# Reordered units and a sorting copy with its step on the write side, in a kernel of a long convolution and a linear attention

## Chip, cores and metric

The kernel runs on one core of a Trainium2 chip. The metric is the device time of one execution in microseconds, given as the median of several runs; a shorter name below for an engine is PE (TensorE), ACT (ScalarE), DVE (VectorE), POOL (GpSimd) and SP (SyncE, whose queue issues every DMA here).

## What is computed

Two independent heads over S = 2048 time points and D = 576 columns, in bfloat16, whose results stand side by side in the output.

```python
# A: shift convolution, then a long convolution by FFT
k_shift = sum(k_pad[:, t:t+S] * shift_k[:, 3-t] for t in range(4))   # k padded by 3
kv  = k_shift * v
y   = irfft(rfft(pad(kv)) * rfft(pad(ssm_k)))[:S]                    # length 2S, per column
out_a = q * (y + kv * ssm_D)
# B: linear attention, 32 heads of 18 columns
q, k, v = split(x @ wqkv)
pq, pk = phi(q), phi(k)              # phi(t) = (t+1 if t>0 else exp(t)) + 1e-6
kv  = einsum("bhsd,bhse->bhde", pk, v);  z = sum_s pk
out_b = ((pq @ kv) / (pq @ z + 1e-6)) @ wo
out = concatenate([out_a, out_b], -1)
```

## The kernel before, in words

Head A does its Fourier transforms as matmuls, for five chunks of columns (ACH: four of 128, one of 64). Time is split as t = 16a + b, so that a transform is a first step over a (128 points, matrices G), a transposition by DMA, a second step over b (16 points, small matrices W0 and W), a product of spectra, and the way back. The units, each with a name that the lists below use (first number the chunk):

- hl (h_load, L438) loads a chunk of the filter ssm_k, columns on partitions, 2048 time points in a row; hd (h_D, L500) adds D to its first point; hT (h_T, L506) brings time point a to the partitions. hT.0 to hT.2 (mode D) do it with 16 TensorE transposes and one DVE copy. hT.3 (mode a, ACT) and hT.4 (mode p, POOL) first sort the row by b with a copy into hp (L518 to L522), and one DMA transpose from SP (L524) then makes hT.
- cv (L477) is the four-tap shift convolution on DVE or POOL, in stages 0 to 3; each letter of its mode is the engine of one operation.
- h1 and u1 (s1, L527) are the first transform step of the filter and of the signal: 8 matmuls into a PSUM bank and an eviction (L308 on ACT, L310 on DVE) into Ch or Cu. ht and ut (tr, L540) transpose them by DMA into Cth and Ctu. h2 and u2 (s2, L548) are the second step, evicted into T and SU.
- pX, pT, pS, pA (prod, L563) are the product of the spectra on DVE or POOL; the mode N leaves a fold out, and i1 then takes more matmuls. i1 (L580) and i2 (L599) go back, with F, which FT (f_T, L610) makes from G by a DMA transpose. st stores.
- sin, ix, io, iw, iv, sw, wk and W make the matrices G and W from sines at the start; wm (one_w, L359) fills a row of the weights with two memsets (L361, L362).

Head B: xl loads x, xd transposes it (PE, or SP with mode T), k, q and qt are the projections (5 matmuls each half, an exp on ACT at L447, a min/max on DVE at L448), G (b_G, L657) is pk^T x with 32 matmuls, whose eviction needs a column that DVE copies first (L651) before ACT evicts (L652); zs, zz, kv, M, den (with the reciprocal, L743), bc and bt (L745, L755; they divide pq by the denominator, on DVE), and o and ol for the output.

The order of all this is written out by hand as a string, ORDER: one word per unit, with a trailing letter for the engine that evicts, and behind the slash the places (buffer slots and one of four PSUM bank pairs, 0 to 3). Each unit's instructions are put on the queues of their engines in this order, and every engine, SP included, works its queue in order. A unit waits for its bank until the eviction of the last unit there is done. Filter rows, hp and hT share one ring of three slots ("h"), Cth and Ctu one of two ("ct").

Of the kernel before, what the change touches and what calls it, by code (L numbers as in the profile page):

```python
# [29 lines left out]


ORDER = """
io ls ix.0.0/0 sin.1.0 wu.1.A/0 wu.2.B/1 dl ix.1.0/1 sin.0.0 hl.0/0 dc/2 hd.0 Wj.A/301 ix.0.1 id xl.2 iw ix.1.1 sin.0.1
hl.1/1 hT.0.D/22 xd.2.DA/030 hd.1 h1.0.0.0.A/11 h1.0.1.0.D/2 hT.1.D/00 wm iv sin.1.1 xl.0 h1.0.0.1.A/3 xd.0.DA/112
h1.0.1.1.A/0 wk lw.1 sw W lw.2 k.11/3 hl.2/1 hd.2 lw.0 k.9/2 k.2/0 k.1/1 k.10/3 kl.0 h1.1.1.1.A/02 k.8/0 cv.0.0.D es
cv.0.1.DD hc h1.1.1.0.A/1 h1.1.0.1.A/3 q.2.1/2 xl.3 q.0.1/0 k.0/1 h1.1.0.0.A/3 ht.0.0/0 qt.0/2 ht.0.1/1 h2.0.1.1.A/00
cv.0.2.PD vl.0/0 cv.0.3.DDD h2.0.1.0.A/3 eps ql.0/1 q.2.0/1 hl.3/2 xd.3.AA/020 q.0.0/3 k.3/2 ht.1.1/1 u1.0.1.1.A/10
k.15/1 u1.0.1.0.A/3 hT.2.D/00 u1.0.0.1.A/2 u1.0.0.0.A/1 cv.1.0.P cv.1.1.DD k.13/3 cv.1.2.DD h2.1.1.1.A/10 h2.1.1.0.A/2
q.3.1/1 h2.0.0.1.A/20 xd.1.T/1 h2.0.0.0.A/3 cv.1.3.DDP q.3.0/2 ut.0.0/1 u2.0.0.0.A/00 q.1.0/3 k.7/1 k.6/0 FT.0.T
u2.0.0.1.A/2 ut.0.1/0 pX.0.0.D/0 qt.1/3 u2.0.1.0.A/11 u2.0.1.1.D/0 k.12/2 u1.1.1.0.A/11 kl.1 k.5/3 u1.1.0.1.A/0  # L40
pX.0.1.D/1 k.14/1 ht.1.0/1 xl.1 u1.1.0.0.A/2 u1.1.1.1.A/3 cv.2.0.D hl.4/1 pT.0.1.D k.4/0 h1.2.1.0.A/02 pS.0.1.D ut.1.1/0
h1.2.1.1.A/1 cv.2.1.DD pT.0.0.P hd.3 pS.0.0.D q.1.1/3 h2.1.0.0.A/32 h2.1.0.1.A/0 G.1/1 cv.2.2.DP h1.2.0.0.A/2 pA.0.1.N
h1.2.0.1.D/0 u2.1.1.1.A/03 zs/01 ut.1.0/1 u2.1.1.0.A/2 pA.0.0.N i1.0.0.0.D/10 i1.0.0.1.A/3 i1.0.1.0.A/1 zz/2
i1.0.1.1.A/0 pX.1.1.D/0 vl.1/0 cv.2.3.DDD ht.2.0/0 pT.1.1.D u2.1.0.1.A/13 u2.1.0.0.A/2 ht.2.1/1 FT.1.T hT.3.a/02 hd.4
G.3/1 cv.3.0.D cv.3.1.DD u1.2.0.0.A/00 lwv pS.1.1.D u1.2.1.1.A/3 G.0/2 cv.3.2.DD u1.2.1.0.A/1 pX.1.0.D/1 pA.1.0.N
u1.2.0.1.A/0 G.4/3 h2.2.1.1.A/22 cv.3.3.DDD h2.2.1.0.A/1 G.2/0 cv.4.0.D i2.0.0/3 h2.2.0.0.A/02 h2.2.0.1.A/1 wom kv/0
ut.2.0/1 i2.0.1/3 h1.3.0.0.A/12 h1.3.1.0.A/1 h1.3.0.1.D/0 h1.3.1.1.A/3 pA.1.1.P ut.2.1/0 u2.2.0.0.D/02 i1.1.1.1.A/01
i1.1.1.0.A/0 u2.2.0.1.A/3 pT.1.0.D cv.4.1.DD den/2 u2.2.1.1.A/11 pS.1.0.N i1.1.0.1.A/0 i1.1.0.0.A/3 lwo M.3.A/1 M.2.A/0
i2.1.1/3 u2.2.1.0.A/1 i2.1.0/0 ht.3.1/1 h2.3.1.1.A/12 hT.4.p/02 u1.3.1.1.A/01 bc.2/32 u1.3.0.1.A/0 u1.3.0.0.A/1 bt/3
M.1.A/0 u1.3.1.0.A/2 h2.3.1.0.D/1 ht.3.0/0 h2.3.0.1.A/33 bc.0/02 st.0 ut.3.0/1 h1.4.1.0.A/11 h1.4.0.1.A/3 h1.4.1.1.A/1  # L50
h2.3.0.0.A/0 bc.3/31 pX.2.0.P/0 pT.2.0.P M.4.A/2 ut.3.1/0 pX.2.1.P/1 h1.4.0.0.A/0 M.0.A/3 bc.1/20 pA.2.0.N pT.2.1.D
pS.2.1.D u2.3.0.0.A/01 u2.3.0.1.A/3 pS.2.0.P cv.4.2.PD cv.4.3.DDD i1.2.0.1.A/02 i1.2.0.0.A/1 ht.4.0/1 pX.3.0.D/0 ql.1/1
o.1.2.AAf/03 pA.2.1.P i1.2.1.1.A/2 o.0.2.AA/10 u1.4.0.0.D/13 i1.2.1.0.D/2 u1.4.1.0.A/1 h2.4.0.1.A/03 u1.4.1.1.D/0
u1.4.0.1.A/1 u2.3.1.1.A/12 u2.3.1.0.A/3 ut.4.0/0 pT.3.0.D h2.4.0.0.A/0 i2.2.1/1 pX.3.1.D/1 pA.3.1.D pS.3.0.D pA.3.0.P
o.1.0.AA/23 pT.3.1.D o.0.0.AAf/10 u2.4.0.0.A/02 u2.4.0.1.D/3 i1.3.0.1.A/11 i2.2.0/0 i1.3.0.0.A/2 st.1 pX.4.0.D/0
pT.4.0.D pA.4.0.D pS.3.1.P i1.3.1.0.A/3 pS.4.0.D i1.3.1.1.A/1 o.1.3.AAs/02 i2.3.0/3 i1.4.0.0.A/01 i1.4.0.1.D/0 i2.3.1/2
o.0.3.DAs/31 i2.4.0/0 i2.4.1/2 st.2 o.1.1.AA/31 ol.0.1/023
"""


# [192 lines left out]
def kernel(  # L253
# [52 lines left out]
    def evict(out, in_, eng):  # L306
        if eng == 'A':
            nc.scalar.activation(out=out, in_=in_, func=ACT.Copy)  # L308
        else:
            nc.vector.tensor_copy(out=out, in_=in_)  # L310
# [195 lines left out]
    def h_T(ci, eng='D'):  # L506
        d0, dc = ACH[ci]
        s = st[ci]
        hv = s['h'][0:dc, :].rearrange("d (a b) -> d b a", b=16)
        if eng in 'DAH':  # L510
            s['hT'] = slot4([128, 16, 128], BF, "hT", "h", 3)
            for b0, n, e in ((0, 8, 'A'), (8, 8, 'D')) if eng == 'H' else ((0, 16, eng),):
                ps = psum.tile([128, n, 128], BF, name="hT_ps")
                for b in list(range(1, n)) + [0]:
                    nc.tensor.transpose(out=ps[:, b, 0:dc], in_=hv[:, b0 + b, :], identity=K.ident[0:dc, 0:dc])
                evict(s['hT'][:, b0:b0 + n, 0:dc], ps[:, :, 0:dc], e)
        else:
            hp = slot4([128, 16, 128], BF, "hp", "h", 3)[0:dc]  # L518
            if eng == 'a':
                nc.scalar.activation(out=hp, in_=hv, func=ACT.Copy)  # L520
            else:
                nc.gpsimd.tensor_copy(out=hp, in_=hv)  # L522
# [372 lines left out]
```

## Time and profile before

| | us |
|---|---|
| median of three runs | 158.77 (158.46 to 159.52) |
| the profiled execution | 159.33 |
| its span, first to last instruction | 157.6 |
| PE busy | 149.6 (95%) |
| DVE busy | 135.8 (86%) |
| ACT busy | 130.5 (83%) |
| POOL busy | 62.0 (39%) |
| ACT's sorting copy (hT.3), one | 4.02 |
| POOL's sorting copy (hT.4, half the partitions), one | 3.93 |

The profile is one execution. Times in its timelines count from the span's start; a row of a timeline is start, length, engine, line, operation, output<-input, shape and count, and in brackets the idle time of the engine before it and what ended that. A row of groups is line, engine, operation, shapes and count, then busy time and mean of one in ns, then idle time before it with its cause.

### The profile page before, as it was taken

The numbers are of one execution on the slowest core, as the hardware profiler recorded it, in microseconds if no ns is written. First come the engines' busy times: TensorE is split into PE (matmuls) and PEld (weight loads), VectorE is DVE, ScalarE is ACT, GpSimd is POOL, SyncE is SP. The second block draws the span as 40 slices with busy tenths as digits, with TensorE's granted clock in tenths as the row PEclk, the third lists the DMA queues.
The fourth block names the chain that finished last, engine by engine and source line by source line (L and its number), as shares of the span: only waits on it lengthen the run. The fifth ranks groups of instructions, "written<-read, shape, count | busy, mean of one in ns | idle before, by whom it ended". The sixth has DMA issues, their size and how long they took to land.

```text
span 157.6 us, 4600 instructions
## 1 busy us (share of the span) xinstructions
PE 149.6 (95%) x1986; PEld 90.3 (57%) x1986; DVE 135.8 (86%) x169; ACT 130.5 (83%) x162; POOL 62.0 (39%) x70
## 2 busy tenths in 40 slices
...
GB/s 86 391 282 188 294 300 186 253 290 266 184 186 225 127 317 264 143 213 324 177 176 176 209 109 144 192 141 146 263 170 148 131 319 186 173 107 189 0 227 198
DMA packets 74315, 31.92 MB, mean 203 GB/s; under 512 B 52090, under 2 KB 73653, under 8 KB 74294
## 3 DMA queue, kind: packets, MB, share of 16 engines
...
q14 instruction: 6, 0.05, 0.1%
...
## 4 chain that ended last, share of the span: by engine, by line
PE 77%; ACT 12%; DMA 3%; DVE 3%; issue 1%; POOL 1%; DVEq 0%; POOLq 0%; ACTq 0%
PE k_ps L455 12%; PE g_ps L661 10%; PE o_ps L783 9%; PE s_ps L536 8%; PE q_ps L464 8%; PE i_ps L593 6%; PE s_ps L559 5%; DMA Ctu<-Cu 3%; PE i_ps L606 3%; PE i_ps L607 2%; ACT V L308 2%; ACT T L308 2%; ACT Cu L308 2%; PE o_ps L775 2%; ACT G L231 2%; PE qt_ps L472 2%
## 5 line engine op out<-in xcount | busy, mean ns | idle before, releaser
L455 PE MATMUL k_ps<-wqk,xT 128*128 128x512 bf16 (+1 forms) x160 | 21.5, 286 | 0.0
L536 PEld LDWEIGHTS <-G 128*128 128x128 bf16 x320 | 17.4, 98 | 3.6 <-issue 2.7
L464 PE MATMUL q_ps<-xT,wqk 128*128 128x512 bf16 x80 | 18.4, 380 | 0.0
L308 ACT ACTIVATE Cu<-s_ps 128x1024 bf16<-128x1024 f32 (+1 forms) x18 | 17.0, 976 | 0.4 <-PE s_ps L536 0.2
L455 PEld LDWEIGHTS <-xT 128*128 128x128 bf16 x160 | 11.4, 98 | 10.5 <-issue 0.3
L308 ACT ACTIVATE T<-s_ps 128x1024 bf16<-128x1024 f32 x17 | 16.8, 1026 | 0.6 <-PE s_ps L559 0.6
L308 ACT ACTIVATE ob<-o_ps 128x576 bf16<-128x576 f32 (+1 forms) x15 | 9.2, 637 | 9.1 <-PE o_ps L775 4.8
L661 PE MATMUL g_ps<-pk,x_sb 128*128 128x512 bf16 (+1 forms) x128 | 16.5, 286 | 0.0
L308 ACT ACTIVATE Ch<-s_ps 128x1024 bf16<-128x1024 f32 (+1 forms) x17 | 15.2, 928 | 1.0 <-PE s_ps L536 1.0
L494 DVE TENSOR_TENSOR at<-at 128x2048 bf16<-128x2048 bf16 (+1 forms) x14 | 15.5, 1109 | 0.5
L308 ACT ACTIVATE SU<-s_ps 128x1024 bf16<-128x1024 f32 x15 | 15.0, 1040 | 1.0 <-PE s_ps L559 1.0
L308 ACT ACTIVATE V<-i_ps 128x1024 bf16<-128x1024 f32 x15 | 14.7, 1039 | 1.0 <-PE i_ps L593 1.0
L783 PE MATMUL o_ps<-wo_M,pqT 128*128 128x512 bf16 (+1 forms) x112 | 14.9, 286 | 0.0
L448 DVE SCALAR_TENSOR_TENSOR pk<-pk,k_ps 128x576 bf16<-128x576 bf16 x16 | 11.8, 751 | 3.4 <-ACT pk L447 3.3
L493 DVE TENSOR_TENSOR at<-k,Wj 128x2048 bf16<-128x2048 bf16 (+1 forms) x13 | 14.7, 1134 | 0.1
L661 PEld LDWEIGHTS <-x_sb 128*128 128x128 bf16 x128 | 8.4, 97 | 8.9 <-issue 1.2
L447 ACT ACTIVATE pk<-k_ps,neg 128x576 bf16<-128x576 f32 x16 | 11.6, 741 | 1.3 <-PE k_ps L455 0.9
L464 PEld LDWEIGHTS <-wqk 128*128 128x128 bf16 x80 | 7.4, 98 | 9.1 <-issue 1.3
L608 DVE TENSOR_TENSOR q<-i_ps,q 128x1024 bf16<-128x1024 f32 (+1 forms) x10 | 10.9, 1105 | 1.9 <-PE i_ps L607 1.8
L783 PEld LDWEIGHTS <-pqT 128*128 128x128 bf16 x112 | 7.5, 98 | 7.7 <-issue 0.9
L536 PE MATMUL s_ps<-hT,G 128*128 128x128 bf16 (+1 forms) x160 | 10.7, 216 | 1.0 <-ACT G L231 0.4
L593 PE MATMUL i_ps<-W,T 64*128 64x128 bf16 x160 | 11.3, 217 | 0.4 <-DVE pqT L753 0.4
...
## 6 DMA issues: line engine op xcount, KB each, us to landing
...
```

Of the source, the lines that this page charges most:

```text
L308: nc.scalar.activation(out=out, in_=in_, func=ACT.Copy)
L447: nc.scalar.activation(out=out_ap, in_=ps_ap, func=ACT.Exp, bias=K.neg1[0:n, :])
L448: nc.vector.scalar_tensor_tensor(out=out_ap, in0=out_ap, scalar=1.0, in1=ps_ap, op0=ALU.min, op1=ALU.max)
L455: nc.tensor.matmul(ps[:, n0:n1], lhsT=xT[r // 4][:, t, rr * 128:(rr + 1) * 128], rhs=wqk[:, t, D + n0:D + n1], start=(t == 0), stop=(t == 4))
L464: nc.tensor.matmul(ps[:, j, :], lhsT=wqk[:, t, 128 * c:128 * c + 128], rhs=xT[g][:, t, :], start=(t == 0), stop=(t == 4))
L493: on[0].tensor_tensor(out=t_, in0=kk[:, 3 - stage:19 - stage], in1=wb(stage), op=ALU.mult)
L494: on[1].tensor_tensor(out=a_, in0=a_, in1=t_, op=ALU.add)
L536: nc.tensor.matmul(ps[:, bi, 0:dc], lhsT=K.G[ri][:, b, :], rhs=xf(b), start=True, stop=True)
L593: nc.tensor.matmul(ps[:, r, g, :], lhsT=s[key, hf][64 * r:64 * r + 64, z, x, 128 * g:128 * g + 128], rhs=K.W[64 * r:64 * r + 64, m, :], st ...
L608: nc.vector.tensor_tensor(out=qs, in0=ps[:, :, 0:dc], in1=qs, op=ALU.mult)
L661: nc.tensor.matmul(ps[:, n0:n1], lhsT=x_sb[:, r, f0:f0 + fn], rhs=pk[:, r, n0:n1], start=(r == 0), stop=(r == 15))
L783: nc.tensor.matmul(pss[i][:, n0:n1], lhsT=pqT[:, c, r * 128:(r + 1) * 128], rhs=B['M'][:, c, n0:n1], start=(c == 0 and not first), stop=(c ...
```

## The change

First, the copy: the same elements go to the same places, but the loop over them runs along the source, a outer and b inner, so that it reads the row in sequence and writes with a step of 128 elements. Before, it ran along the destination, and read with a step of 16.

```diff
             hp = slot4([128, 16, 128], BF, "hp", "h", 3)[0:dc]
+            h_in, h_out = s['h'][0:dc, :].rearrange("d (a b) -> d a b", b=16), hp.rearrange("d b a -> d a b")
             if eng == 'a':
-                nc.scalar.activation(out=hp, in_=hv, func=ACT.Copy)
+                nc.scalar.activation(out=h_out, in_=h_in, func=ACT.Copy)
             else:
-                nc.gpsimd.tensor_copy(out=hp, in_=hv)
+                nc.gpsimd.tensor_copy(out=h_out, in_=h_in)
```

Second, ORDER is replaced by one with the same 296 units. The first lines and those from G.3 to the output, old and new:

```diff
-io ls ix.0.0/0 sin.1.0 wu.1.A/0 wu.2.B/1 dl ix.1.0/1 sin.0.0 hl.0/0 dc/2 hd.0 Wj.A/301 ix.0.1 id xl.2 iw ix.1.1 sin.0.1
-hl.1/1 hT.0.D/22 xd.2.DA/030 hd.1 h1.0.0.0.A/11 h1.0.1.0.D/2 hT.1.D/00 wm iv sin.1.1 xl.0 h1.0.0.1.A/3 xd.0.DA/112
-h1.0.1.1.A/0 wk lw.1 sw W lw.2 k.11/3 hl.2/1 hd.2 lw.0 k.9/2 k.2/0 k.1/1 k.10/3 kl.0 h1.1.1.1.A/02 k.8/0 cv.0.0.D es
...
-G.3/1 cv.3.0.D cv.3.1.DD u1.2.0.0.A/00 lwv pS.1.1.D u1.2.1.1.A/3 G.0/2 cv.3.2.DD u1.2.1.0.A/1 pX.1.0.D/1 pA.1.0.N
...
-M.1.A/0 u1.3.1.0.A/2 h2.3.1.0.D/1 ht.3.0/0 h2.3.0.1.A/33 bc.0/02 st.0 ut.3.0/1 h1.4.1.0.A/11 h1.4.0.1.A/3 h1.4.1.1.A/1
-h2.3.0.0.A/0 bc.3/31 pX.2.0.P/0 pT.2.0.P M.4.A/2 ut.3.1/0 pX.2.1.P/1 h1.4.0.0.A/0 M.0.A/3 bc.1/20 pA.2.0.N pT.2.1.D
...
+io ls ix.0.0/0 ix.1.0/1 wu.1.A/0 sin.1.0 id wu.2.B/1 dl sin.0.0 ix.0.1 ix.1.1 hl.0/0 wm dc/2 hd.0 Wj.A/301 sin.0.1 iw
+hT.0.D/12 xl.2 hl.1/2 hd.1 xd.2.DA/030 xl.0 sin.1.1 hT.1.D/01 h1.0.0.0.A/12 h1.0.1.0.D/0 h1.0.0.1.A/3 h1.0.1.1.D/1 iv
+xd.0.DA/120 lw.1 sw wk lw.2 W k.11/3 hc k.9/1 hl.4/2 kl.0 k.1/0 k.10/2 k.8/3 h1.1.1.1.A/01 lw.0 es eps h1.1.0.1.A/0
...
+pX.1.1.D/0 pT.1.1.D u1.2.1.1.A/03 u1.2.0.0.A/0 G.0/1 u1.2.0.1.A/2 u1.2.1.0.A/3 pA.1.1.D pS.1.1.D cv.3.2.DD G.4/0
...
+ht.3.0/1 bc.2/31 u1.3.0.0.A/2 h2.3.1.0.A/3 st.0 bt/0 u1.3.1.0.A/2 M.1.A/1 bc.0/30 h2.3.0.1.A/32 h1.4.0.1.A/11
+h1.4.1.0.A/3 h1.4.1.1.D/2 h2.3.0.0.A/1 bc.3/03 h1.4.0.0.A/2 M.4.A/1 M.0.A/2 bc.1/01 u2.3.0.0.A/03 ut.3.1/1
...
```

What it comes to, engine by engine:

- SP: the load hl.4 (chunk 4) goes out ninth, where hl.2 stood; hl.2 goes out behind ql.0, where hl.3 stood; hl.3 goes out behind ut.0.0, where FT.0 stood. kl.0 now precedes lw.0, and ht.0.0 precedes xl.3. FT.1 and FT.0 go out one behind the other, behind the transpose of hT.3; lwv goes out before ht.2.0; ut.2.1 precedes ut.2.0 and hT.4 precedes ht.3.1.
- DVE: wm, id and all of ix stand ahead of the copy of hT.0. cv.3.0 and cv.3.1 stand ahead of G.3's column copy, and pX.1.1, pT.1.1 behind it; cv.4.0 and pX.1.0 stand later.
- ACT: hd.2 moves from behind k.11 to behind k.15, hd.4 to before the last two SU evictions of chunk 1; sin.1.1 stands ahead of the first Ch eviction.
- PE: the same units, most of them in the same place; hT.1 ahead of the first h1, i2.0.0 behind the last two h2 of chunk 2, and many neighbours exchanged.
- Evictions from ACT to DVE: h1.0.1.1, u2.1.1.0, i1.0.0.1, h1.4.1.1, the first half of o.0.2, h2.4.0.0, the second of o.1.1. From DVE to ACT: i1.0.0.0, h2.3.1.0, u1.4.0.0, i1.4.0.1. From POOL to DVE: pA.1.1, pA.2.1, pA.3.0. From DVE to POOL: the first operation of cv.4.1, the second of cv.4.2, pT.3.0.
- The PSUM banks and the slots of the rings are assigned anew.

More of the change, by code (lines that the diff above doesn't have):

```diff
@@ L32 @@
 ORDER = """
-io ls ix.0.0/0 sin.1.0 wu.1.A/0 wu.2.B/1 dl ix.1.0/1 sin.0.0 hl.0/0 dc/2 hd.0 Wj.A/301 ix.0.1 id xl.2 iw ix.1.1 sin.0.1
-hl.1/1 hT.0.D/22 xd.2.DA/030 hd.1 h1.0.0.0.A/11 h1.0.1.0.D/2 hT.1.D/00 wm iv sin.1.1 xl.0 h1.0.0.1.A/3 xd.0.DA/112
-h1.0.1.1.A/0 wk lw.1 sw W lw.2 k.11/3 hl.2/1 hd.2 lw.0 k.9/2 k.2/0 k.1/1 k.10/3 kl.0 h1.1.1.1.A/02 k.8/0 cv.0.0.D es
-cv.0.1.DD hc h1.1.1.0.A/1 h1.1.0.1.A/3 q.2.1/2 xl.3 q.0.1/0 k.0/1 h1.1.0.0.A/3 ht.0.0/0 qt.0/2 ht.0.1/1 h2.0.1.1.A/00
-cv.0.2.PD vl.0/0 cv.0.3.DDD h2.0.1.0.A/3 eps ql.0/1 q.2.0/1 hl.3/2 xd.3.AA/020 q.0.0/3 k.3/2 ht.1.1/1 u1.0.1.1.A/10
@@ L38 @@
[L38 to L42, printed above, removed]
@@ L43 @@
-h1.2.0.1.D/0 u2.1.1.1.A/03 zs/01 ut.1.0/1 u2.1.1.0.A/2 pA.0.0.N i1.0.0.0.D/10 i1.0.0.1.A/3 i1.0.1.0.A/1 zz/2
-i1.0.1.1.A/0 pX.1.1.D/0 vl.1/0 cv.2.3.DDD ht.2.0/0 pT.1.1.D u2.1.0.1.A/13 u2.1.0.0.A/2 ht.2.1/1 FT.1.T hT.3.a/02 hd.4
-G.3/1 cv.3.0.D cv.3.1.DD u1.2.0.0.A/00 lwv pS.1.1.D u1.2.1.1.A/3 G.0/2 cv.3.2.DD u1.2.1.0.A/1 pX.1.0.D/1 pA.1.0.N
-u1.2.0.1.A/0 G.4/3 h2.2.1.1.A/22 cv.3.3.DDD h2.2.1.0.A/1 G.2/0 cv.4.0.D i2.0.0/3 h2.2.0.0.A/02 h2.2.0.1.A/1 wom kv/0
-ut.2.0/1 i2.0.1/3 h1.3.0.0.A/12 h1.3.1.0.A/1 h1.3.0.1.D/0 h1.3.1.1.A/3 pA.1.1.P ut.2.1/0 u2.2.0.0.D/02 i1.1.1.1.A/01
@@ L48 @@
-i1.1.1.0.A/0 u2.2.0.1.A/3 pT.1.0.D cv.4.1.DD den/2 u2.2.1.1.A/11 pS.1.0.N i1.1.0.1.A/0 i1.1.0.0.A/3 lwo M.3.A/1 M.2.A/0
-i2.1.1/3 u2.2.1.0.A/1 i2.1.0/0 ht.3.1/1 h2.3.1.1.A/12 hT.4.p/02 u1.3.1.1.A/01 bc.2/32 u1.3.0.1.A/0 u1.3.0.0.A/1 bt/3
-M.1.A/0 u1.3.1.0.A/2 h2.3.1.0.D/1 ht.3.0/0 h2.3.0.1.A/33 bc.0/02 st.0 ut.3.0/1 h1.4.1.0.A/11 h1.4.0.1.A/3 h1.4.1.1.A/1
-h2.3.0.0.A/0 bc.3/31 pX.2.0.P/0 pT.2.0.P M.4.A/2 ut.3.1/0 pX.2.1.P/1 h1.4.0.0.A/0 M.0.A/3 bc.1/20 pA.2.0.N pT.2.1.D
-pS.2.1.D u2.3.0.0.A/01 u2.3.0.1.A/3 pS.2.0.P cv.4.2.PD cv.4.3.DDD i1.2.0.1.A/02 i1.2.0.0.A/1 ht.4.0/1 pX.3.0.D/0 ql.1/1
@@ L53 @@
[L53 to L57, printed above, removed]
+io ls ix.0.0/0 ix.1.0/1 wu.1.A/0 sin.1.0 id wu.2.B/1 dl sin.0.0 ix.0.1 ix.1.1 hl.0/0 wm dc/2 hd.0 Wj.A/301 sin.0.1 iw
@@ new lines @@
+hT.0.D/12 xl.2 hl.1/2 hd.1 xd.2.DA/030 xl.0 sin.1.1 hT.1.D/01 h1.0.0.0.A/12 h1.0.1.0.D/0 h1.0.0.1.A/3 h1.0.1.1.D/1 iv
+xd.0.DA/120 lw.1 sw wk lw.2 W k.11/3 hc k.9/1 hl.4/2 kl.0 k.1/0 k.10/2 k.8/3 h1.1.1.1.A/01 lw.0 es eps h1.1.0.1.A/0
+cv.0.0.D cv.0.1.DD k.2/2 h1.1.1.0.A/3 ht.0.0/0 xl.3 q.2.1/1 q.0.1/0 k.0/3 cv.0.2.PD ht.0.1/1 h1.1.0.0.A/2 qt.0/1 vl.0/0
+cv.0.3.DDD ql.0/1 h2.0.1.0.A/00 h2.0.1.1.A/2 q.2.0/3 xd.3.AA/001 q.0.0/2 u1.0.1.1.A/10 k.3/1 k.15/3 hl.2/1 hd.2
+u1.0.1.0.A/0 hT.2.D/02 cv.1.0.P cv.1.1.DD u1.0.0.1.A/1 ht.1.1/1 u1.0.0.0.A/3 xd.1.T/1 k.13/0 h2.1.1.1.A/12 cv.1.2.DD
```

17 lines of the change are left out of this document (added).

## The prediction

> **What bounds the kernel now.** I read the page first (busy shares), then the table by stages, then TensorE's timeline for the places where it stops, and last the timelines of the engine or queue that each stop names.
>
> ```profile
> span 157.6 us, 4600 instructions
> ...
> PE 149.6 (95%) x1986; PEld 90.3 (57%) x1986; DVE 135.8 (86%) x169; ACT 130.5 (83%) x162; POOL 62.0 (39%) x70
> ...
> GB/s 86 391 282 188 294 300 186 253 290 266 184 186 225 127 317 264 143 213 324 177 176 176 209 109 144 192 141 146 263 170 148 131 319 186 173 107 189 0 227 198
> ```
>
> ```profile
> 40.00:48.00 8.00, 7.38 (x70) 3.03 (x67) 7.86 (x8) 7.46 (x9) 0.52 (x1) 1.00 1.02 165
> 104.00:112.00 8.00, 7.45 (x107) 4.84 (x102) 8.00 (x6) 7.14 (x9) 7.92 (x3) 1.00 0.91 147
> 112.00:120.00 8.00, 7.45 (x103) 3.46 (x101) 7.20 (x7) 7.10 (x11) 8.00 (x4) 0.80 0.97 214
> ```
>
> ```profile
> 42.01 0.62 PE L559 MATMUL s_ps<-Cth,W 64*32 64x512 bf16 x16 [0.34 <-DMA Cth<-Ch]
> 48.24 0.41 PE L559 MATMUL s_ps<-Ctu,W 64*32 64x512 bf16 x8 [0.52 <-DMA Ctu<-Cu]
> 120.78 0.23 PE L593 MATMUL i_ps<-W,T 64*128 64x128 bf16 x2 [0.36 <-DVE pqT L753]
> ```
>
> TensorE is busy for 149.6 of 157.6 us, so all that any order can win is the other 8 us and the work done at a lower clock. The columns of the second fence are stage, its length, busy time of PE, PEld, DVE, ACT and POOL, then the granted clock, DMA share and GB/s. Two kinds of stage lose time in the middle: 40 to 49, where two transposed tiles come late over DMA (0.34 and 0.52 us), and 104 to 121, where VectorE is busy for all of 8.00 us, TensorE loses 0.55 us in each row, one more 0.36 us at 120.78, and the clock falls to 0.80. The change leaves the number of matmuls alone: every inverse-transform unit i1 still stands behind the same folded products, so TensorE's work is the same and only its stops can move.
>
> **The copy.** Two chunks are sorted by a copy, hT.3 on ScalarE and hT.4 on GpSimd.
>
> ```profile
> L520 ACT ACTIVATE hp<-h_sb 128x2048 bf16<-128x2048 bf16 x1 | 4.0, 4023 | 0.0
> ...
> L308 ACT ACTIVATE xT<-xT_ps 128x2048 bf16<-128x2048 bf16 x1 | 1.9, 1869 | 0.0
> ```
>
> ```profile
> 82.72 0.76 ACT L652 ACTIVATE wv_GT<-g_ps,ex 128x576 bf16<-128x576 f32 x1
> ```
>
> ```profile
> L522 POOL COPY hp<-h_sb 64x2048 bf16<-64x2048 bf16 x1 | 3.9, 3927 | 0.0
> ```
>
> The same number of elements without a step takes ScalarE 1.87 us, so the new copy lies between 1.87 (the step of the reads was the cost) and 4.02 (the step costs as much in the writes); I take 2.0, because ScalarE's other evictions write with steps already: Cu (written with steps) and SU (contiguous) both take 1.02 to 1.04 us.
>
> ```profile
> L308 ACT ACTIVATE Cu<-s_ps 128x1024 bf16<-128x1024 f32 x16 | 15.8, 1023 | 0.4 <-PE s_ps L536 0.2
> L308 ACT ACTIVATE SU<-s_ps 128x1024 bf16<-128x1024 f32 x15 | 15.0, 1040 | 1.0 <-PE s_ps L559 1.0
> ```
>
> What the 2 us buy is another matter. The next ScalarE instruction is the eviction of G.3 (L652, now at 82.72), and it needs a column that VectorE copies first (L651). In the new order VectorE does that copy behind cv.3.0 and cv.3.1, three conv steps, and its queue is continuous from zz, which ends at 75.38 (L704): three steps of cv.2.3, then these three, some 7.2 us by the group below (1.13 us, and the waits for one's own result between two of them), and L651 at 82.8. So ScalarE waits there until 82.9 with a short copy or a long one.
>
> ```profile
> 75.06 0.32 DVE L704 TENSOR_TENSOR zsel<-hsel,z_ps 128x160 bf16<-128x160 bf16 x1 [0.42 <-PE z_ps L702]
> ```
>
> ```profile
> L493 DVE TENSOR_TENSOR at<-k,Wj 128x2048 bf16<-128x2048 bf16 (+1 forms) x13 | 14.7, 1134 | 0.1
> ```
>
> I cost the copy at nothing on both engines. The cover on ScalarE is that wait; if L651 came at once, the 2 us would reach the evictions of u1.2, but TensorE is fully busy there and has free banks, so it would still be worth nothing. What follows hT.3 on SP now counts: its transpose is followed by both transposes of F (FT.1, FT.0), moved here, each 2.5 us of SP time by the row of F further down. From a copy that ends at 81, hT.3's transpose (2.2, as for Ctu) and FT.1 stand ahead; FT.0 is issued at 85.7 and lands 4.7 us later, at 90.4, needed by i2.0.0 at about 93. With a 4.0 us copy it lands at 92.4, still in time. GpSimd's copy (3.93 us) lies in idle time of an engine that is 39% busy, and its tile belongs to the last chunk.
>
> ```profile
> DMA to landing us min/median/max: 4.7/4.7/4.7
> ```
>
> ```profile
> 92.73 0.22 PE L606 MATMUL i_ps<-V,F 128*128 128x128 bf16 x1
> ```
>
> By the Trainium skill, page "SBUF — State Buffer", section "Door 1: The DMA port swizzle", in its note on cachelines, an access that lands on a new 16-byte line each time pays a penalty. Read strictly this speaks against the change: elements written with a step of 256 bytes pay what the reads paid, and the copy stays at 4.0 us. The Cu row does not bear that out for runs of 4 bytes; no row shows runs of 2. The sum is the same either way; it is rival C.
>
> **The start.** Two memsets of wqk (unit wm) move ahead of the first hT copy on VectorE, and the fourth s1 eviction (h1.0.1.1) moves from ScalarE to VectorE.
>
> ```profile
> 7.12 1.22 DVE L310 COPY hT<-hT_ps 128x2048 bf16<-128x2048 bf16 x1
> ...
> 11.26 1.21 DVE L310 COPY hT<-hT_ps 128x2048 bf16<-128x2048 bf16 x1
> 12.53 0.54 DVE L361 MEMSET wqk<- 64x576 int32 x1
> 13.24 0.54 DVE L362 MEMSET wqk<- 1x576 int32 x1 [0.17 <-DVE wqk L361]
> 13.71 0.57 DVE L207 TENSOR_SCALAR sm<-sm 128x448 int32<-128x448 int32 x1
> ```
>
> ```profile
> 12.96 6.39 PE L455 MATMUL k_ps<-wqk,xT 128*128 128x512 bf16 x50
> ```
>
> The memsets take 1.25 us (12.53 to 13.78). The hT copy then starts at 8.25 instead of 7.12, and behind it stand five evictions at some 1.17 us (hT.0, xT.2, hT.1, two s1), to 14.1. L207 follows, so it is 0.4 us later; the sine on ScalarE (L236) waits for it and the exps of all first k units stand behind that. On TensorE the s1 units run into the same queue: the fourth waits for the hT.1 copy at 11.75, and the first k unit starts near 13.3 instead of 12.96. I take +0.4; ends 0 (the bias add of chunk 2, 0.3 us, leaves ScalarE's queue there) and +0.8.
>
> **The loads and SP's queue, 11 to 48 us.** The load of chunk 4 (256 KB) takes the place of chunk 2's (512 KB) at 11.11, chunk 2's that of chunk 3's at 30.02, and FT.0 leaves its place behind the first Ctu.
>
> ```profile
> 11.11 0.35 SPq L442 DMA_DIRECT2D h_sb<-in_A_ssm_k_dram  x1
> ...
> 30.02 3.52 SPq L442 DMA_DIRECT2D h_sb<-in_A_ssm_k_dram  x1
> 33.72 4.65 SPq L543 DMA_TRANSPOSE Cth<-Ch  x1
> ...
> 41.61 1.25 SPq L340 DMA_TRANSPOSE xT<-in_B_x_dram  x1
> 43.02 2.17 SPq L543 DMA_TRANSPOSE Ctu<-Cu  x1
> 45.23 2.53 SPq L613 DMA_TRANSPOSE F<-G  x1
> ```
>
> ```profile
> DMA to landing us min/median/max: 3.5/6.5/8.8
> ```
>
> ```profile
> 40.03 1.94 ACT L308 ACTIVATE Cu<-s_ps 128x1024 bf16<-128x1024 f32 x2 [0.23 <-PE s_ps L536]
> ```
>
> Ahead of the Cth transpose at 33.72 there are 256 KB less. The seven slices from 15.8 to 43.4 us (3.94 us each) move 294 to 184 GB/s, about 250, so 256 KB are 1.0 us. The Cth that TensorE waited for at 42.01 comes 1 us sooner: its 0.34 us go. The Ctu is bound twice: by SP, whose x transposes end their issue at 42.86, and by the four Cu evictions, the last of which ends at 41.97 and inherit the +0.4 of the start. Its issue falls from 43.02 to between 42.4 and 43.0, its landing (48.2 now) to 47.6 to 48.2, and TensorE comes for it at about 47.8. So 0.1 to 0.5 of the 0.52 us go; I take 0.3. Sum here -0.64, ends 0 and -0.86. What is queued behind chunk 2's load: its bias add (hd.2) now stands on ScalarE ahead of three Cu evictions, right after the exp of k.15, which ends at 38.88.
>
> ```profile
> 38.14 0.74 ACT L447 ACTIVATE pk<-k_ps,neg 128x576 bf16<-128x576 f32 x1
> ```
>
> The longest landing of the h loads, 8.8 us, is that of the one issued at 30.02 (landing 38.8); 1 us sooner it is there at 37.8, wanted at 39.3.
>
> **The bc stage, 104 to 122 us.** The eviction of h2.3.1.0 goes from VectorE to ScalarE, that of h1.4.1.1 (half the columns) the other way.
>
> ```profile
> 113.01 1.23 DVE L310 CAST T<-s_ps 128x1024 bf16<-128x1024 f32 x1
> 114.15 4.66 DVE L753 SCALAR_TENSOR_TENSOR pqT<-pqT,bc_ps 128x1024 bf16<-128x1024 bf16 x4
> 119.51 2.35 DVE L753 SCALAR_TENSOR_TENSOR pqT<-pqT,bc_ps 128x1024 bf16<-128x1024 bf16 x2 [0.69 <-PE bc_ps L749]
> ```
>
> VectorE, which sets the pace here, loses 1.15 us and gains about 0.6; ScalarE the reverse. The last bc then ends up to 0.6 us earlier and the stop at 120.78 shrinks. ScalarE has 0.9 us idle in each of the two 8-us rows, so it takes the 0.4 us. I take -0.4, ends 0 and -0.8.
>
> **The rest.** From 56 to 104 the new neighbours swap inside a row of units with the same eviction time, and TensorE is full: 0, ends -0.2 and +0.5. From 122 on only who evicts changes, the last pieces are the same: 0, ends -0.3 and +0.5.
>
> **Sum.** +0.4 - 0.64 - 0.4 = -0.6 us. The profiled execution took 159.33 us (span 157.6 and 1.7 around it), so it would take 158.7; it was 0.56 above the median of the three runs, 158.77, and the same -0.6 there gives **158.2 us**. About 1% (1.6 us) is what a measurement of this kernel can tell from no change.
>
> **Rivals.**
>
> A: *the clock does not fall.* The table in steps of 2 us shows where the 0.80 comes from.
>
> ```profile
> 116.00:118.00 2.00, 1.98 (x25) 0.90 (x18) 2.00 (x3) 1.84 (x3) 2.00 (x2) 0.71 0.95 196
> 118.00:120.00 2.00, 2.00 (x24) 0.66 (x22) 1.31 (x2) 1.25 (x3) 2.00 (x2) 0.50 1.11 210
> 120.00:122.00 2.00, 1.64 (x60) 1.31 (x46) 2.00 (x3) 1.83 (x3) 1.38 (x1) 0.94 0.43 84
> ```
>
> The clock falls behind a stretch of short stops: 0.29 x 2 + 0.50 x 2 + 0.06 x 2 = 1.7 us of TensorE's work are lost, which at half clock is a stretch of 3.4 us. The path loses up to 1.7 us by it, and at least the 0.69 us for which VectorE waits for bc. If the new order leaves fewer stops before it, -1.2 more: 157.0. For it: VectorE's load there falls, and the three runs spread by 1.06 us, about one such event. Against it: my walk of banks and evictions leaves as many short stops (ScalarE gets the eviction). [...]
>
> B: *chunk 2 comes late* (slower). If its load at SP's old place of chunk 3 lands after 39.3 instead of 37.8, hd.2 holds ScalarE, three Cu evictions, the Ctu transpose and TensorE's hT.2 behind it, one for one. Landing at 41.5 gives +2.2 and the second stall back: 160.7. For it: the queue there was already saturated (3.52 us for one issue). Against it: 256 KB less ahead.
>
> C: *the copy is no faster*: it ends at 83 instead of 81, under the same wait for L651, and FT.0 has 0.6 us of its margin left: 158.2 as well. For it: no row of before writes single elements with a step. The Trainium skill's 16-byte rule gives this case.
>
> **Chances.** Forecast 0.50, A 0.27, B 0.15, C 0.08. Faster by over 1% (below 157.2): most of A (0.21) and the lower tail of the forecast (0.09), 0.30. Slower by over 1% (above 160.4): most of B (0.12) and the upper tails of forecast and C (0.05), 0.17. Within 1%: 0.53. The forecast's own range, from the ends, is 157.0 to 159.6; with most of A and half of B, 156.2 to 160.5.
>
> **What would show it.** Right: L520 at 2.0 to 2.2 us with idle time of ScalarE behind it, waiting for ex L651; the first k unit near 13.3; no stop at s_ps<-Cth near 42 and a smaller one at Ctu; the last bc near 121.2. Wrong: a wait of ScalarE at L504 for h_sb near 39; a TensorE stop at L606 near 93 on F; the first k unit at 13.0 or at 14; a gain above 2 us without a change of the clock rows.

## The result, and the profile after

The changed kernel takes **177.4 us** (median of four runs, 176.25 to 178.69) against 158.9 (158.46 to 159.52) for the kernel before, run beside it: ratio 1.116, 95% interval 1.106 to 1.126. It is 18.5 us slower, where the prediction said 0.6 us faster. The profiled execution took 178.69 us. Ratios here leave disturbed runs out and medians do not, so that the two can differ by half a per cent.

The first lines of the page of the changed kernel:

```profile
span 177.0 us, 4600 instructions
...
PE 154.4 (87%) x1986; PEld 94.8 (54%) x1986; DVE 150.3 (85%) x172; ACT 134.8 (76%) x159; POOL 70.6 (40%) x70
```

The number of matmuls is the same, as forecast, but TensorE is no longer busy all the time: the span grew by 19.4 us and its busy time by only 4.8. It stops three times for over 2 us, once behind ScalarE's sorting copy and twice behind GpSimd's. The instructions that write hp (line, operation, shortest/median/longest in ns, start; the copy's two lines are now L521 and L523, other lines below L520 count one more than before):

```profile
L521 ACT ACTIVATE hp<-h_sb x1: 9377/9377/9377, 80.7 to 80.7; 128x2048 bf16<-128x2048 bf16 x1
L523 POOL COPY hp<-h_sb x1: 10016/10016/10016, 101.5 to 101.5; 64x2048 bf16<-64x2048 bf16 x1
```

They took 4.02 and 3.93 us before. What each of them does to the rest is read from the timelines of the changed kernel. **ScalarE's copy** first: ScalarE's own row of work, and TensorE's row that waits for it.

```profile
80.70 9.38 ACT L521 ACTIVATE hp<-h_sb 128x2048 bf16<-128x2048 bf16 x1
89.56 0.99 ACT L653 ACTIVATE wv_GT<-g_ps,ex 128x576 bf16<-128x576 f32 x1
```

```profile
90.60 0.61 PE L537 MATMUL s_ps<-v,G 128*128 128x128 bf16 x8 [3.41 <-ACT wv_GT L653]
```

The eviction of G.3 stands behind the copy. No idle time is left ahead of it, so the wait that was to cover the copy is gone; TensorE's next unit waits for this eviction, a stop of 3.41 us.

**GpSimd's copy**: GpSimd's row and VectorE's row over the same stretch, then TensorE's two stops.

```profile
101.45 10.02 POOL L523 COPY hp<-h_sb 64x2048 bf16<-64x2048 bf16 x1
111.07 2.28 POOL L493 TENSOR_TENSOR at<-k,Wj 128x1024 bf16<-128x1024 bf16 x1
113.32 4.04 POOL L572 TENSOR_TENSOR X<-SU,T 128x2048 bf16<-128x2048 bf16 x1
117.43 4.92 POOL L574 TENSOR_TENSOR T<-SU,T 128x2048 bf16<-128x2048 bf16 x1
```

```profile
107.27 1.23 DVE L310 CAST SU<-s_ps 128x1024 bf16<-128x1024 f32 x1
108.41 2.97 DVE L491 TENSOR_TENSOR at<-k,Wj 128x1024 bf16<-128x1024 bf16 x1
111.31 7.13 DVE L574 TENSOR_TENSOR T<-SU,T 128x2048 bf16<-128x2048 bf16 x1
118.36 4.54 DVE L494 TENSOR_TENSOR at<-at 128x1024 bf16<-128x1024 bf16 x1
```

```profile
118.50 0.40 PE L594 MATMUL i_ps<-W,T 64*128 64x128 bf16 x4 [8.03 <-DVE T L574]
...
127.28 0.22 PE L607 MATMUL i_ps<-V,F 128*128 128x128 bf16 x1 [2.12 <-DVE Gz L744]
```

Three operations of VectorE that have both inputs in SBUF (cv.4.0, pT.1.0, the sum of cv.4.1) stretch to 2.97, 7.13 and 4.54 us. Each ends by a GpSimd instruction beside it: the first with the copy (111.4), the second 1.1 us, its own time, after pX.2.0 (117.4; GpSimd's cv.4.1 and pX.2.0 had followed the copy without a gap), the third 0.55 us after pT.2.0 (122.35), which VectorE had kept out in turn (4.92 us instead of 4.07). VectorE is then still late with the reciprocal (L744), for which TensorE stops a second time. The cast just ahead reads PSUM and takes 1.23 us beside the copy, as ever. In the kernel before the same work fell into a gap of GpSimd:

```profile
95.68 3.93 POOL L522 COPY hp<-h_sb 64x2048 bf16<-64x2048 bf16 x1
102.89 4.06 POOL L571 TENSOR_TENSOR X<-SU,T 128x2048 bf16<-128x2048 bf16 x1 [3.28 <-ACT SU L308]
```

```profile
100.43 1.22 DVE L573 TENSOR_TENSOR T<-SU,T 128x2048 bf16<-128x2048 bf16 x1
101.56 0.68 DVE L493 TENSOR_TENSOR at<-k,Wj 128x1024 bf16<-128x1024 bf16 x1
```

GpSimd was idle from 99.6 to 102.9, and pT.1.0 took 1.22 us and the half-size conv steps 0.68 there. By these durations the changed kernel's VectorE loses (2.97 - 0.68) + (7.13 - 1.22) + (4.54 - 0.68) = 12.1 us.

The table by stages of the changed kernel (stage, length, busy time of PE, PEld, DVE, ACT, POOL, granted clock, DMA share, GB/s) shows what the two longest stops cost on top:

```profile
92.00:96.00 4.00, 3.70 (x30) 2.12 (x30) 0.00 (x0) 2.80 (x4) 0.00 (x0) 0.57 1.13 230
...
116.00:120.00 4.00, 1.50 (x30) 1.51 (x32) 4.00 (x2) 1.02 (x1) 3.92 (x2) 0.50 0.34 65
120.00:124.00 4.00, 4.00 (x57) 2.98 (x54) 3.86 (x4) 2.84 (x4) 2.35 (x1) 0.61 0.00 0
```

In these rows TensorE works at about half clock: 3.70 x 0.43 = 1.6 us are lost behind the first, 1.50 x 0.50 + 4.00 x 0.39 = 2.3 us behind the second. With the stops that is 3.4 + 1.6 = 5.0 us for ScalarE's copy and 8.0 + 2.3 + 2.1 = 12.4 us for GpSimd's.

### The profile page after: what moved, and what is told of

Read it like the earlier page. It is cut to its first block, busy times and chain, and to the rows that moved or that the text cites. A ratio compares the mean times of both kernels' runs of the same rounds, so it can differ in the third digit from the quotient of the medians.

```text
span 177.0 us, 4600 instructions
## 1 busy us (share of the span) xinstructions
PE 154.4 (87%) x1986; PEld 94.8 (54%) x1986; DVE 150.3 (85%) x172; ACT 134.8 (76%) x159; POOL 70.6 (40%) x70
## 4 chain that ended last, share of the span: by engine, by line
PE 67%; DVE 11%; ACT 7%; issue 7%; DMA 6%; ACTq 0%; DVEq 0%
PE k_ps L455 10%; PE o_ps L784 8%; PE q_ps L464 7%; PE g_ps L662 6%; PE s_ps L537 6%; PE i_ps L594 5%; ACT Cu L308 5%; PE s_ps L560 4%; DMA Cth<-Ch 3%; DMA Ctu<-Cu 3%; DVE at L494 3%; PE hT_ps L515 2%; PE warm_ps L79 2%; PE g_ps L667 2%; PE i_ps L607 2%
## 5 line engine op out<-in xcount | busy, mean ns | idle before, releaser
L594 PE MATMUL i_ps<-W,T 64*128 64x128 bf16 x160 | 12.9, 237 | 8.5 <-DVE T L574 8.0
L494 DVE TENSOR_TENSOR at<-at 128x2048 bf16<-128x2048 bf16 (+1 forms) x13 | 18.7, 1438 | 0.4
L308 ACT ACTIVATE V<-i_ps 128x1024 bf16<-128x1024 f32 x16 | 16.0, 1030 | 4.0 <-PE i_ps L594 3.3
L464 PE MATMUL q_ps<-xT,wqk 128*128 128x512 bf16 x80 | 18.5, 380 | 0.0
L574 POOL TENSOR_TENSOR T<-SU,T 128x2048 bf16<-128x2048 bf16 x3 | 13.0, 4348 | 11.6 <-DVE X L572 11.6
L308 ACT ACTIVATE Ch<-s_ps 128x1024 bf16<-128x1024 f32 (+1 forms) x15 | 13.5, 938 | 1.4 <-PE s_ps L537 1.4
L308 ACT ACTIVATE ob<-o_ps 128x576 bf16<-128x576 f32 (+1 forms) x13 | 8.0, 635 | 7.6 <-PE o_ps L776 4.4
L537 PE MATMUL s_ps<-v,G 128*128 128x128 bf16 (+1 forms) x160 | 10.4, 214 | 3.9 <-ACT wv_GT L653 3.4
L594 PEld LDWEIGHTS <-T 64*128 64x128 bf16 x160 | 8.2, 104 | 10.4 <-DVE T L574 8.7
L574 DVE TENSOR_TENSOR T<-SU,T 128x2048 bf16<-128x2048 bf16 x6 | 13.2, 2206 | 0.1
L594 PE MATMUL i_ps<-W,X 64*128 64x128 bf16 x208 | 13.0, 231 | 0.0
```

The source lines that it names most:

```text
L464: nc.tensor.matmul(ps[:, j, :], lhsT=wqk[:, t, 128 * c:128 * c + 128], rhs=xT[g][:, t, :], start=(t == 0), stop=(t == 4))
L494: on[1].tensor_tensor(out=a_, in0=a_, in1=t_, op=ALU.add)
L537: nc.tensor.matmul(ps[:, bi, 0:dc], lhsT=K.G[ri][:, b, :], rhs=xf(b), start=True, stop=True)
L574: e.tensor_tensor(out=t[:], in0=s['SU', hf][:], in1=t[:], op=ALU.mult)
L594: nc.tensor.matmul(ps[:, r, g, :], lhsT=s[key, hf][64 * r:64 * r + 64, z, x, 128 * g:128 * g + 128], rhs=K.W[64 * r:64 * r + 64, m, :], st ...
```

## The experiments

Theory C: the two copies are the whole loss, ScalarE's through the evictions behind it, GpSimd's through VectorE (theory L: the two exclude each other where both read SBUF). Rival O: the new order has its part in it. Runs 5 to 8 and 11 are one execution each.

**1. The order alone**: the new ORDER, with the copy as it was.

```diff
-            h_in, h_out = s['h'][0:dc, :].rearrange("d (a b) -> d a b", b=16), hp.rearrange("d b a -> d a b")
-                nc.scalar.activation(out=h_out, in_=h_in, func=ACT.Copy)
+                nc.scalar.activation(out=hp, in_=hv, func=ACT.Copy)
-                nc.gpsimd.tensor_copy(out=h_out, in_=h_in)
+                nc.gpsimd.tensor_copy(out=hp, in_=hv)
```

> New order, both copies in their old form (reads with a step, writes in sequence). Theory C (the copy's step on the write side costs, 9.4 us on ScalarE and 10.0 on GpSimd where 4.0 and 3.9 stood, and all else follows from these two): copies back at 4.0 and 3.9 us, no TensorE stop of over 1 us between 80 and 125, 157 to 160.5 us. Rival O (the order itself costs most of the 18.5 us, since it sets GpSimd's work beside VectorE's on 104 to 124): 168 us or more, with the long VectorE operations L574 and L494 still there.

Measured: 159.46 us (158.27 to 162.13, ten runs) against 158.44; ratio 1.0035, interval 0.9995 to 1.0075. Rival O falls. The profiled execution of this run (158.63 us, span 156.9) lets the prediction's steps on the order be read without the copies. TensorE, VectorE and ScalarE of this run:

```profile
13.25 3.04 PE L455 MATMUL k_ps<-wqk,xT 128*128 128x512 bf16 x21
...
41.78 0.63 PE L559 MATMUL s_ps<-Cth,W 64*32 64x512 bf16 x16
...
47.42 0.41 PE L559 MATMUL s_ps<-Ctu,W 64*32 64x512 bf16 x8
```

```profile
116.36 4.63 DVE L753 SCALAR_TENSOR_TENSOR pqT<-pqT,bc_ps 128x1024 bf16<-128x1024 bf16 x4
```

```profile
77.93 3.98 ACT L520 ACTIVATE hp<-h_sb 128x2048 bf16<-128x2048 bf16 x1
82.18 0.74 ACT L652 ACTIVATE wv_GT<-g_ps,ex 128x576 bf16<-128x576 f32 x1 [0.27 <-DVE ex L651]
```

The first k unit starts at 13.25, neither Cth nor Ctu has a stop, and the last bc ends at 121.0. GpSimd's old copy takes 4.61 us in this order, not the 3.9 expected: it starts at 93.42, 0.4 us behind VectorE's pX.1.0 (93.02, 1.21 us long, both inputs in SBUF). ScalarE's two rows matter most: with the old copy, ScalarE is 0.27 us early for G.3. All the cover there was for a longer copy is 0.27 us.

**2. The copy alone**: the old ORDER with the new copy.

```diff
+            h_in, h_out = s['h'][0:dc, :].rearrange("d (a b) -> d a b", b=16), hp.rearrange("d b a -> d a b")
-                nc.scalar.activation(out=hp, in_=hv, func=ACT.Copy)
+                nc.scalar.activation(out=h_out, in_=h_in, func=ACT.Copy)
-                nc.gpsimd.tensor_copy(out=hp, in_=hv)
+                nc.gpsimd.tensor_copy(out=h_out, in_=h_in)
```

> Old order, both copies in the new form. Theory C: copies at 9.4 and 10 us; ScalarE's delays the evictions behind it by 5.4 us, GpSimd's ends near 106 and holds VectorE's pT.1.0; 167 to 175 us. Rival O: under 163 us.

Measured: 178.94 us (177.98 to 179.06), ratio 1.127, interval 1.121 to 1.133; more than the 167 to 175 expected, and no less than the whole change costs.

```profile
L523 POOL COPY hp<-h_sb x1: 9372/9372/9372, 102.2 to 102.2; 64x2048 bf16<-64x2048 bf16 x1
```

```profile
106.98 9.43 DVE L574 TENSOR_TENSOR T<-SU,T 128x2048 bf16<-128x2048 bf16 x1
```

With no such VectorE operation at its start GpSimd's new copy takes 9.37 us, as ScalarE's does, so some 0.65 of the 10.02 belong to the order. pT.1.0 takes 9.43 us.

**3. and 4. One copy at a time**: the new ORDER, with the new form of the copy on ScalarE alone (the first pair of lines of the diff above), then on GpSimd alone (the second pair).

> New order, only ScalarE's copy (chunk 3) in the new form, GpSimd's in the old one. Theory C: ScalarE's copy 9.4 us, the TensorE stop of some 3.4 us and the two of 0.3 us behind it near 90 stay, and half-clock work behind them; 4 to 7 us over the kernel with the new order and old copies, 162 to 166 us. Rival O: within 2 us of the full change, 177.

> New order, only GpSimd's copy (chunk 4) in the new form, ScalarE's in the old one. Theory C: GpSimd's copy 10 us; VectorE's L491, L574 and L494 at 3, 7 and 4.5 us as in the full change; 9 to 13 us over the kernel with the new order and old copies, 168 to 172 us. Rival O: within 2 us of 177. If the two halves do not add up to the whole, the two costs share a part.

Measured: 165.97 us on ScalarE alone, ratio 1.0438 (1.0362 to 1.0514); 170.97 us on GpSimd alone, ratio 1.0764 (1.0699 to 1.083). Over the order alone that is 0.0403 and 0.0729, and 1.0035 + 0.0403 + 0.0729 = 1.1167 is the ratio of the whole change, 1.1164. In us (of 158.4) the two copies cost 6.4 and 11.5, near the 5.0 and 12.4 of stops and lowered clock above. Each has its own stop; TensorE's rows, first of the run with ScalarE's copy, then of that with GpSimd's:

```profile
90.16 1.91 PE L537 MATMUL s_ps<-v,G 128*128 128x128 bf16 x16 [3.39 <-ACT wv_GT L653]
```

```profile
111.14 0.40 PE L594 MATMUL i_ps<-W,T 64*128 64x128 bf16 x4 [8.06 <-DVE T L574]
```

**5. A long copy without the new form**: the kernel before, with GpSimd's old copy issued twice, 3.9 us more of GpSimd's reads and nothing else.

```diff
                 nc.gpsimd.tensor_copy(out=hp, in_=hv)
+                nc.gpsimd.tensor_copy(out=hp, in_=hv)
```

> Old order, old form, GpSimd's sorting copy issued twice (same result), so that GpSimd copies from 95.7 to 103.5 instead of 99.6. Theory L (GpSimd and those VectorE operations that have two SBUF inputs shut each other out for a whole instruction): pT.1.0 on VectorE (L573, 1.22 us, now from 100.4 to 101.65, and it waits for no GpSimd result) lasts until the second copy ends, some 3 us, while VectorE operations with a PSUM input beside the copies keep their length (L608 and L310 at 1.20 to 1.23). Rival D (GpSimd's lateness reaches VectorE only through data): pT.1.0 stays at 1.22 us. The Trainium skill, page SBUF — State Buffer, section Who interferes with whom, has the first rule.

Measured: 170.2 us, against 158.17 beside it. GpSimd and VectorE:

```profile
99.61 3.94 POOL L523 COPY hp<-h_sb 64x2048 bf16<-64x2048 bf16 x1
103.52 4.04 POOL L572 TENSOR_TENSOR X<-SU,T 128x2048 bf16<-128x2048 bf16 x1
107.63 4.92 POOL L574 TENSOR_TENSOR T<-SU,T 128x2048 bf16<-128x2048 bf16 x1
```

```profile
100.38 8.27 DVE L574 TENSOR_TENSOR T<-SU,T 128x2048 bf16<-128x2048 bf16 x1
108.56 4.53 DVE L493 TENSOR_TENSOR at<-k,Wj 128x1024 bf16<-128x1024 bf16 x1
```

The theory was right in kind and far too mild, with some 3 us expected for pT.1.0: 3.9 us more of GpSimd cost 12 us. pT.1.0 missed the gap, which the second copy filled; the copy runs into pX.2.0 without a pause, and VectorE gets in only at 107.6, when pX.2.0 ends. Its next operation then sits out pT.2.0.

**11. The same length with nothing read**: the kernel before, with four memsets behind GpSimd's copy, into the tile that the transpose then overwrites.

```diff
             s['hT'] = slot4([128, 16, 128], BF, "hT", "h", 3)
+            for _ in range(4 if eng == 'p' else 0):
+                nc.gpsimd.memset(s['hT'][:].rearrange("p b a -> p (b a)").bitcast(I32), 0)
```

> The kernel before, with four memsets of 128x1024 words on GpSimd right behind its copy (into the tile that the transpose then overwrites), 4.1 us in all: as long as the second copy of the run with the copy issued twice, but with nothing read. Theory L (VectorE and GpSimd exclude each other where both read SBUF): VectorE's pT.1.0 at about 100.4 takes 1.2 us as before, and the time is 157.5 to 159.5. Rival Q (any GpSimd instruction keeps such VectorE work out, or the delay comes through GpSimd's queue): pT.1.0 takes 4 to 8 us and the time is 165 to 171. Between them: VectorE slips in between two memsets, pT.1.0 takes 1.5 to 2.5 us, 158 to 160.

Measured: 159.07 us (159.09 beside it). GpSimd and VectorE:

```profile
99.84 3.98 POOL L525 MEMSET hT<- 128x1024 int32 x4
103.79 4.06 POOL L573 TENSOR_TENSOR X<-SU,T 128x2048 bf16<-128x2048 bf16 x1
```

```profile
100.72 1.22 DVE L575 TENSOR_TENSOR T<-SU,T 128x2048 bf16<-128x2048 bf16 x1
```

GpSimd is as busy and its queue as late as with the second copy, and pT.1.0 takes its 1.22 us in the middle of the memsets. So it is GpSimd's reads of SBUF that keep out a VectorE operation with two inputs in SBUF, not its being busy. The Trainium skill, page "SBUF — State Buffer", section "Who interferes with whom", states just this: such a VectorE instruction contends with a GpSimd instruction that reads SBUF and not with one that only writes it, and the loser is blocked for the whole instruction. These two runs agree, with 8.27 against 1.22 us. VectorE was even kept out for longer than one instruction, over the rest of the copy and all of pX.2.0.

**6. and 7. Between the two forms**: the kernel before, with copies that write runs of 2, then of 8 elements (the two copies take h_out and h_in as in run 2; for runs of 8, r=8).

```diff
+            h_in, h_out = s['h'][0:dc, :].rearrange("d (g r b) -> d g b r", r=2, b=16), hp.rearrange("d b (g r) -> d g b r", r=2)
```

> Old order; both copies write runs of 2 elements (4 bytes), blocks of 2 time points inside the loop over the 16 places, so that reads alternate between two lines. If the price of the step is one per run written: some 5.5 to 7 us on ScalarE, between 4.0 (old form) and 9.4 (new form). If any step on the write side costs the full price: 9.4 us. If runs of 2 are already free, as the stepped evictions (Cu) suggested: 4.0 us or less.

> Old order; both copies write runs of 8 elements (16 bytes). If the price is one per run written: 4.0 to 4.7 us on both engines, as in the old form, whose reads it shares. If any step on the write side costs: well above 5 us.

Measured: 158.23 and 158.43 us (158.17 beside them). The copies, with runs of 2, then ScalarE's with runs of 8:

```profile
L521 ACT ACTIVATE hp<-h_sb x1: 2191/2191/2191, 78.3 to 78.3; 128x2048 bf16<-128x2048 bf16 x1
L523 POOL COPY hp<-h_sb x1: 2102/2102/2102, 95.4 to 95.4; 64x2048 bf16<-64x2048 bf16 x1
```

```profile
L521 ACT ACTIVATE hp<-h_sb x1: 4040/4040/4040, 78.5 to 78.5; 128x2048 bf16<-128x2048 bf16 x1
```

The length of the run does not act smoothly: 9.4 us with single elements, 2.2 with pairs, 4.0 with runs of 8. The 2.2 falls under "4.0 us or less", but no expectation had pairs beat the old form; the next run takes the forms apart.

**8. The forms by themselves**: twelve copies of one tile of zeros behind the end of the kernel before, to tiles that nobody reads, with nothing else at work but ScalarE and GpSimd side by side.

> The kernel before with 12 further copies of one 128x2048 tile of zeros behind its last unit, which go to tiles that nobody reads: ScalarE does seven, GpSimd five, in this order: contiguous; write with a step of 256 bytes (the new form); write with a step of 32 bytes; read with a step of 32 bytes (the old form); pairs (runs of 2 elements written); on ScalarE also a write of 2-byte elements with a step of 4 bytes, and a write of 4-byte elements with a step of 256 bytes. Theory H (half words: what costs is a write of a single 2-byte element that does not go on in the same 4-byte word, whatever the step): ScalarE 1.9, 9.4, 9.4, 4.0, 2.2, 9.4, and about 2 for the 4-byte elements. Theory S (what costs is the size of the step): 1.9, 9.4, between 4 and 9, 4.0, 2.2, 2 for the step of 4 bytes, and 9.4 for the 4-byte elements at 256 bytes. Theory K (contention: the copy is slow because other engines and DMA move data beside it): with nothing beside it the new form takes 2 to 4. GpSimd the same in kind. The whole takes some 35 us longer than before; that time tells nothing.

ScalarE, in the order of the expectation (the fourth column names the engine, L885 and L886 are the last two forms):

```profile
154.85 1.91 ACT L884 ACTIVATE d<-src 128x2048 bf16<-128x2048 bf16 x1 [0.44 <-DVE src L871]
156.79 10.39 ACT L884 ACTIVATE d<-src 128x2048 bf16<-128x2048 bf16 x1
167.22 8.87 ACT L884 ACTIVATE d<-src 128x2048 bf16<-128x2048 bf16 x1
176.12 3.87 ACT L884 ACTIVATE d<-src 128x2048 bf16<-128x2048 bf16 x1
180.03 2.16 ACT L884 ACTIVATE d<-src 128x2048 bf16<-128x2048 bf16 x1
182.07 2.46 ACT L885 ACTIVATE d<-src 128x2048 bf16<-128x2048 bf16 x1
184.57 3.64 ACT L886 ACTIVATE d<-src 128x2048 f32<-128x2048 bf16 x1
```

GpSimd's five are within 0.04 us of ScalarE's; its new form:

```profile
156.83 10.40 POOL L888 COPY p<-src 128x2048 bf16<-128x2048 bf16 x1
```

Theory K (contention) falls: with the rest of the core idle the new form takes 10.4 us. The two engines did run side by side here, but in the changed kernel ScalarE's copy (80.7 to 90.1) took 9.38 us while GpSimd stood idle, as GpSimd's next row there shows:

```profile
100.93 0.58 POOL L644 MEMSET wo_M<- 128x576 int32 x1 [23.51 <-PE g_ps L662]
```

Theory H as worded falls, since single elements at a step of 4 bytes take 2.46 us. Theory S as worded falls too, since 4-byte elements at a step of 256 bytes take 3.64 us and not 9. What is left for the writes needs both: a single 2-byte element, written far from the last one (32 bytes are far, 4 are not, and nothing between was run). At 32 bytes it costs 8.87 / 2048 = 4.3 ns, at 256 bytes 5.1; a 4-byte element at 256 bytes costs 1.8, a read at 32 bytes 1.9, and a pair 2.16 / 1024 = 2.1 for both its elements. Pairs therefore make half as many far writes, each at about the price of a whole word. Their reads are still single elements, which alternate between two places 32 bytes apart, and yet the copy takes 2.16 us where reads that go on by 32 bytes take 3.87; so the distance alone does not price a read either. Why half a word written far away costs more than twice a whole one, and why alternating reads cost next to nothing, stays open.

**9. and 10. The copy in pairs, timed**: the new ORDER and the old one, each with the copies of run 6.

> The changed kernel with its copy in pairs (runs of 2 elements written, inner loop over b, innermost over the pair). If the two slow copies are the whole loss: copies of 2.2 and 2.1 us, no stop of TensorE above 0.6 us between 80 and 125 us, and a time like the new order with the old copy, 158.0 to 159.5. If the new order gains what I forecast for it (0.6 us) once the copies are out of the way, ratio 0.994 to 0.998; rival (covered: the copies of 4 us stood in idle time, and the order is neutral): ratio 0.998 to 1.005.

> The kernel before with the copy in pairs. Covered (forecast: cost of the copy at nothing, in either direction): 158.0 to 159.0, ratio 0.997 to 1.003, though the copies are 1.8 us shorter each. Rival (the copies of 4 us did hold up evictions or VectorE): ratio below 0.997.

Measured beside each other: new order 158.75 us, ratio 0.9966 (0.9931 to 1.0001); old order 158.39 us, ratio 0.9982 (0.9941 to 1.0022). The changed kernel's loss is gone with one other loop order in its copy. Neither version is shown to beat the kernel before: copies of half the length are worth nothing that can be measured, as a copy that ends in idle time should be.

## Why the prediction was wrong

**The failed step is the price of the copy** ("the new copy lies between 1.87 ... and 4.02 (the step costs as much in the writes)"). It measured 9.38 and 10.02. The upper end took for granted that a step costs in the writes what it costs in the reads. Written with a step, 4-byte elements come near that in run 8 (3.64 against 3.87); 2-byte elements are off by a factor of 2.3 to 2.7. The evidence for 2.0 was misread. The prediction took Cu for a write in runs of 4 bytes, but the eviction has b and t innermost, and these lie side by side in the tile, whose dimensions are p, m, z, r, b, t:

```python
            s['C' + key] = slot8([128, 32, 2, 2, 16, 2], BF, "C" + key)
...
        evict(C[:, 0:dc // 4, :, ri, 8 * bg:8 * bg + 8, :].rearrange("p m z b t -> p z m b t"),
```

So Cu is written in runs of 8 x 2 = 16 elements, 32 bytes, and could say nothing of single elements or pairs. The text itself noted that no row showed runs of 2 bytes. The Trainium skill's note on 16-byte lines ("SBUF — State Buffer", "Door 1: The DMA port swizzle"), which I read as a copy that stays at 4.0 and then declined, pointed the right way: 8.87 at 32 bytes against 2.46 at 4 bytes agrees with it in direction, though 3.64 against 10.39, both with a step of 256 bytes, shows that the line alone does not set the price; the size of the element does as much.

**"I cost the copy at nothing on both engines" failed with it**, for two reasons. On ScalarE the cover was named rightly (the wait for L651, forecast until 82.9, found at 82.18) and was good for 4.0 us and 0.27 more. The question what the copy costs if that cover is gone was answered for 2 us only; at 9.4 us the eviction of G.3 began 8.9 us after the copy's start instead of 4.3 (run 1), and TensorE, which was to have free banks, stopped for 3.41 us. On GpSimd "idle time of an engine that is 39% busy" was the wrong view: it asks when GpSimd's own result is needed, and not whom its reads keep out. The cost of GpSimd's copy, 11.5 of some 18 us, went through VectorE, and run 5 shows that 3.9 us more in the old form do the same (12 us). The rivals all moved TensorE's stops by what the order does; none had a slower copy.

Two sums of the prediction do not come out, without bearing on this: 75.38 and 7.2 make 82.6 for L651, not 82.8, and the ends of the terms add up to 156.6 to 160.6, not 157.0 to 159.6.

**The steps on the order** come out in the execution profiled in run 1: first k unit at 13.25 (forecast 13.3), no stop at Cth, last bc at 121.0 (forecast 121.2), span 0.7 us shorter (forecast 0.6). That execution is the second fastest of ten, and luck has a part in it. The timings show no gain: 1.0035 in run 1, with a lower end of 0.9995, leaves no room for the 0.9962 that -0.6 us means; 0.9966 in run 9 does, but its interval reaches 1.0001, and run 10 beside it has 0.9982 with the old order. One reason shows in other executions of the same order. TensorE in the run with GpSimd's new copy (run 4):

```profile
39.26 1.22 PE L515 MATMUL hT_ps<-ident,h_sb 128*128 128x128 bf16 x16 [0.40 <-DMA h_sb<-in_A_ssm_k_dram]
43.02 0.62 PE L560 MATMUL s_ps<-Cth,W 64*32 64x512 bf16 x16 [0.42 <-DMA Cth<-Ch]
```

TensorE's stops on a DMA from 25 to 56 us add up to 0 in run 1, 0.73 in the changed kernel, 0.82 in run 4, 1.40 in run 9 and 1.81 in run 3; in the eight executions profiled with the old order they add up to between 0.23 and 1.86 (0.86 in the one that the prediction read). So the -0.64 for the loads was read from stops that come and go between executions, and no run shows it as the order's. The load of chunk 2 is 0.40, 0.62 and 0.65 us late in three of the five with the new order and in none with the old one, which is rival B at a fifth to a third of its price. The start varies too: the first k unit begins at 12.96 or 12.97 in all eight with the old order, but at 13.24, 13.25, 13.36, 14.89 (the changed kernel) and 15.87 (run 9) with the new one. In the last two TensorE's first 16 transposes take 1.92 and 1.93 us, against 1.21 in run 1; why stays open. Rival A, that the clock does not fall in the bc stage, is what happened in run 1 (granted clock 1.00 from 112 to 120 us), and the runs did not get faster by it. The order does not decide it: the clock is 1.00 there in runs 6, 7, 10 and 11 as well, which have the old one.
